# Key products and the two products that join the block inverses put on 64x64 array tiles, in a gated delta network followed by a softplus MLP

## The chip, the core and the metric

One core of one Trainium2 chip runs the whole program. The core has TensorE (PE; loading of its weights is shown as PEld), VectorE (DVE), ScalarE (ACT), GpSimd (POOL) and SyncE (SP, which here only issues transfers). The time is device microseconds from launch to end; lower is better. Times of a kernel are given as the median of its runs; the profile is of one further execution.

## What is computed

```python
def _attn_ref(q, k, v, beta, g):                  # (4, 8, 768, 48); beta (4, 8, 768)
    k_n = k / (np.linalg.norm(k, axis=-1, keepdims=True) + 1e-06)
    state = np.zeros((B, H, D, D))
    for t in range(S):
        readout = np.einsum('bhd,bhde->bhe', q[:, :, t], state)
        y[:, :, t] = g[:, :, t] * readout
        v_old = np.einsum('bhde,bhd->bhe', state, kt)
        state = state + bt[:, :, :, None] * np.einsum('bhd,bhe->bhde', kt, vt - v_old)

def _moe_ref(x, w_in, w_out):                      # x: (3072, 384); d_ff = 2048
    h = x @ w_in
    g = np.maximum(h, 0.0) + np.log1p(np.exp(-np.abs(h)))
    return g @ w_out
```

x is y with the heads side by side. The kernel does the recurrence in chunks of 64 steps: inside a chunk the updates are the solution of a triangular system, so each chunk and head needs the inverse of a 64x64 unit triangular matrix built from the products of its keys.

## The kernel before

**Chunks and pairs.** S = 768 is cut into NC = 12 chunks of C = 64. There are 4 batches by 8 heads = 32 heads in all; a tile holds 64 steps of two batches on its 128 partitions, and a 64x64 array tile serves one head. Inverses are made for two chunks at a time (a pair, `cc` = 0 to 5), 64 triangular matrices in 32x32 blocks.

**Front** (`front(c, ...)`). `load` and `load_q` bring k, q, v, g of a chunk in two halves of 192 KB each (rings `kf`, `qf`, `vf`, `gf` of 4, 3, 4, 3 buffers). k is normalised (`kmul`), k and q are transposed on PE (`trs`), evicted into `kqt` (`kev`). Then come the key products. For chunks 0 and 1 `gramk` (L405, L406) takes key by key alone and `gramq` (L438) key by query; for the others `gram` (L475, L476) takes both in one product, 32 products on 64x32 array tiles for half a chunk. Each 64x64 key product is written with the columns of the lower half swapped, so that the two diagonal 32x32 blocks of every head stand in `kk[:, 0]` and the others in `kk[:, 1]`. `kkc` evicts them, `mask` evicts the query part.

**Inverse** (`inverse(cc, ...)`). DVE transposes the diagonal blocks (`ln`); POOL (DVE for the first pair) makes the inverses of 16x16 blocks in 15 steps of two operations (`step`). `cv` and `tn` bring one of them, `c16` and `t32` both, back to the block form. Two products join 16x16 blocks to 32x32: `xmm` (L665), 64 products of 16x32 by 16x16 for each chunk, evicted by `xs` in one piece for a pair, and `tmm`, which first copies the diagonal with 4 products by the identity (L686) and adds 64 products of 32x16 by 32x16 (L692), evicted by `td2`. `zmm` (L718, L721) joins 32x32 to 64x64.

**Chain** (`chain(c)`). For each chunk and half of the heads: `ks` and `qs` with the state (L759), `w`, `umm` (L802, L806), `u1`, `zu` (L827), `u2`, then `smm` (L847) and `s` for the next state, `ymm` (L877), `y`, `ytr` (L911), `xt`. These products are small, 16 or 18 at a time, on 64x64 or 32x32 array tiles.

**Dense** (`dense(cs)`). `g1` (L941) takes xt by w_in into `h`, `soft` (ACT) applies softplus, `g2` (L968) takes that by w_out into `o`, evicted and stored. A `g1` or `g2` item is 3, 6 or 4 full-array products. The weights (`wload`, POOL's queue, L273) come in eight parts, w0.0 to w0.3 of w_in and w1.0 to w1.3 of w_out.

**Order.** Nothing reorders at run time. `_ORDER` is a list of entries, an engine's letter and an item's number, and every engine executes its items in that order. A ring's slot is given at an item's place in the list, and an item that needs a slot waits until its last user is done; a load that waits holds up all loads and stores behind it on SP. `pow` (L541) on POOL makes the norms of pairs 1 to 5; `ksq` on ACT squares the keys for them.

Of the kernel before, what the change touches and what calls it, by code (L numbers as in the profile page):

```python
# [74 lines left out]
def kernel(  # L75
# [11 lines left out]
    nc = tc.nc  # L87
# [48 lines left out]
    r_kk = ring("kk", 3, [P, 2, U, HC], F16)  # L136
    r_kqt = ring("kqt", 5, [P, 4 * NP * 2 * C + HC], F16)
# [6 lines left out]
    r_tv = ring("tv", 2, [P, 8, HC, 2], F16)  # L144
    r_tn = ring("tn", 2, [P, U, 16], F16)
    r_xs = ring("xs", 2, [P, U, 16], F16)
# [42 lines left out]
    for t in r_kqt.tiles:  # L189
        nc.vector.memset(t[:, 8 * NP * C :], 0.0)  # L190
    pat = pool.tile([P, HC], F16, name="pat")
    nc.vector.tensor_tensor(pat, ident[:, :HC], ident[:, 64 : 64 + HC], ALU.add)
    for t in r_z.tiles:
        nc.vector.tensor_copy(t[:, :, :HC], pat[:, None, :].broadcast_to([P, 16, HC]))
# [84 lines left out]
    def kq_of(c):  # L279
        return kqt[c].ap[:, : 8 * NP * C].rearrange("p (n t) -> p n t", n=4 * NP)  # L280

    def front(c, kk, nv, nv_it):
# [106 lines left out]
        def u_of(ap, p, m):  # L389
            return ap[:, :, 16 * cl + 8 * p + m : 16 * cl + 8 * p + 8 : 2]  # L390
# [4 lines left out]
        if c < 2:  # L395
            gk = [Buf(p_d), Buf(p_d)]
            for p in range(2):

                def gramk(en, p=p):
                    for i in range(NP):  # L400
                        for r in range(2):
                            for m in range(2):
                                x = kq_u(p, i, r, m)[:, :C]
                                o = gk[m].ap.rearrange("p (n t) -> p n t", n=H)
                                nc.tensor.matmul(o[QUAD[2 * r], NP * p + i], x[:, :HC], x)  # L405
                                nc.tensor.matmul(  # L406
                                    o[QUAD[2 * r + 1], NP * p + i],
                                    x[:, HC:],
                                    x.rearrange("f (x t) -> f x t", x=2)[:, ::-1],
                                )  # L410

                t2 = add("gramk", f"{c}.{p}", "P", gramk, deps=[its["k"][p]],
# [703 lines left out]
```

## Time and profile before

| | us |
|---|---|
| median of 3 runs (lowest, highest) | 302.21 (299.0, 303.22) |
| the profiled execution | 303.66 |
| its span, from the first instruction to the last | 301.7 |

The span is 2 us under the profiled execution's time. Rows of the profile name an engine, a line of the kernel, an operation and its tiles; "idle before" is how long the engine sat idle just before, and the name behind the arrow is what ended that; "issue" there means that nothing the profile shows ended it. PEclk is the clock granted to TensorE as a share of full speed: 1.0 is 2.4 GHz, 0.5 is 1.2 GHz.

### The profile page before, as it was taken

To read this page: it belongs to the slowest core of one execution; us is meant where nothing else is said; L and a number is where in the kernel's file an instruction comes from. 1 tells how busy PE (TensorE), PEld (TensorE's weight loads), DVE (VectorE), ACT (ScalarE), POOL (GpSimd) and SP (SyncE) were. 2 spreads that over 40 slices of the span, in tenths; PEclk is the share of its full clock that TensorE was granted. 3 is DMA by queue.
4 is the path that set the end of the run, shared out by engine and by line. 5 is a ranking of instruction groups with operands and counts; after the bars stand their busy time and mean duration, and the time that the engine had idled before them with its cause. 6 is when DMAs were issued, how large, how long until landed. Compare 5 with 4: busy or idle time off the path is not lost.

```text
span 301.7 us, 13385 instructions
## 1 busy us (share of the span) xinstructions
PE 236.7 (78%) x6112; PEld 161.7 (54%) x6112; DVE 141.0 (47%) x307; ACT 131.7 (44%) x239; POOL 119.7 (40%) x217
## 2 busy tenths in 40 slices
PE   1353239869949976989996996998996999999960
PEld 1233137656737833566653566764564556667730
DVE  7689447824824775374680453553433324112000
ACT  3546245743524764562463523265520355334510
POOL 7204809986361882749868500006820000000000
PEclk9999999977978999799997897798997899999995
DMA  8999998999501099530683012841031110011111
GB/s 126 201 179 186 186 182 141 191 202 161 109 4 30 25 168 163 128 83 8 129 148 69 13 43 65 140 93 31 20 88 32 33 50 9 22 45 39 39 50 42
DMA packets 85480, 27.69 MB, mean 92 GB/s; under 512 B 75568, under 2 KB 85424, under 8 KB 85424
## 3 DMA queue, kind: packets, MB, share of 16 engines
q1 hardware_dynamic: 79376, 23.21, 42.2%
q0 software_dynamic: 3968, 3.25, 7.0%
q8 instruction: 47, 0.77, 1.2%
q10 hardware_dynamic: 2080, 0.39, 0.9%
q14 instruction: 9, 0.07, 0.1%
HBM read 25.26 MB, written 4.72 MB: 99 GB/s over the span
## 4 chain that ended last, share of the span: by engine, by line
PE 70%; DMA 10%; issue 9%; SPq 2%; POOL 2%; ACT 2%; DVE 1%; POOLq 0%; ACTq 0%; DVEq 0%
PE h L941 23%; PE o L968 22%; DMA kf<-in_k_dram 5%; PE d L759 4%; DMA beta_l<-in_beta_dram 3%; PE d L877 2%; PE d L827 2%; DMA out_dram<-osb 2%; PE d L665 2%; PE d L847 2%; PE d L692 2%; PE d L321 2%; PE d L911 2%; PE d L475 2%; PE d L721 1%
## 5 line engine op out<-in xcount | busy, mean ns | idle before, releaser
L941 PE MATMUL h<-xt,w_in 128*128 128x512 f16 (+1 forms) x384 | 78.2, 344 | 1.9 <-ACT ga L953 1.9
L968 PE MATMUL o<-w_out,ga 128*128 128x384 f16 x384 | 75.1, 341 | 0.7 <-ACT osb L200 0.6
L953 ACT ACTIVATE ga<-h 128x512 f16<-128x512 f32 x96 | 57.0, 597 | 37.4 <-PE h L941 35.0
L968 PEld LDWEIGHTS <-ga 128*128 128x128 f16 x384 | 37.6, 102 | 26.6 <-issue 4.6
L941 PEld LDWEIGHTS <-w_in 128*128 128x128 f16 x384 | 36.4, 101 | 24.6 <-issue 5.4
L609 POOL TENSOR_TENSOR tt<-tt,tmp 128x30 f32<-128x30 f32 (+7 forms) x75 | 27.7, 369 | 5.9
L541 POOL TENSOR_TENSOR nv<-nv,half_c 128x32 f32<-128x32 f32 x5 | 27.2, 5449 | 6.6 <-DVE nv L524 6.6
L602 POOL TENSOR_TENSOR tmp<-nn,tt 128x30 f32<-128x30 f32 (+7 forms) x75 | 26.5, 353 | 5.4
L200 ACT ACTIVATE u<-d 128x384 f16<-128x384 f32 x30 | 14.3, 490 | 26.3 <-PE d L806 14.6
L592 POOL TENSOR_TENSOR nn<-ln,beta_l 128x256 f32<-128x256 f16 x10 | 6.0, 619 | 42.9 <-DVE ln L574 42.9
L200 ACT ACTIVATE kqt<-d 128x1024 f16<-128x1024 f16 (+1 forms) x18 | 15.5, 877 | 16.2 <-PE d L321 12.2
L303 POOL TENSOR_TENSOR kn<-kf,nv 128x768 f16<-128x768 f32 x8 | 12.5, 1573 | 19.6 <-DVE nv L547 14.5
L200 ACT ACTIVATE osb<-o 128x384 f32<-128x384 f32 x14 | 6.9, 490 | 29.6 <-PE o L968 24.7
L493 DVE TENSOR_TENSOR mt<-d,mask 128x256 f16<-128x256 f32 x40 | 15.4, 411 | 8.8 <-ACT kk L200 5.4
L892 DVE TENSOR_TENSOR yg<-d,gf 128x384 f16<-128x384 f32 x24 | 12.7, 552 | 14.2 <-PE d L877 14.2
L202 DVE COPY osb<-o 128x384 f32<-128x384 f32 x10 | 5.5, 554 | 28.2 <-PE o L968 28.2
L793 DVE TENSOR_TENSOR w<-vf,d 128x384 f16<-128x384 f32 x22 | 11.1, 547 | 15.4 <-PE d L759 15.4
L759 PE MATMUL d<-s,kqt 48*64 48x48 f16 x704 | 16.2, 195 | 2.1 <-issue 2.1
L665 PE MATMUL d<-tn,kk 16*32 16x16 f16 x768 | 8.6, 171 | 11.8 <-issue 10.6
L202 DVE CAST u<-d 128x384 f16<-128x384 f32 x18 | 9.9, 554 | 16.4 <-PE d L806 8.9
L759 PEld LDWEIGHTS <-kqt 48*64 48x64 f16 x704 | 13.4, 115 | 6.3 <-issue 5.9
L524 DVE TENSOR_REDUCE nv<-ksq 128x16 f32<-128x768 f32 x12 | 11.3, 942 | 10.1 <-ACT ksq L520 10.1
(104 smaller groups left out, 361.7 us busy)
## 6 DMA issues: line engine op xcount, KB each, us to landing
qf<-in_q_dram SPq DMA_DIRECT2D x24, 192.0 KB
vf<-in_v_dram SPq DMA_DIRECT2D x24, 192.0 KB
gf<-in_g_dram SPq DMA_DIRECT2D x24, 192.0 KB
out_dram<-osb SPq DMA_DIRECT2D x24, 192.0 KB
kf<-in_k_dram SPq DMA_DIRECT2D x22, 192.0 KB
w_in<-in_moe_w_in_dram POOLq DMA_DIRECT2D x4, 384.0 KB, 9.0
w_out<-in_moe_w_out_dram POOLq DMA_DIRECT2D x4, 384.0 KB, 8.4
kf<-in_k_dram ACTq DMA_DIRECT2D x2, 192.0 KB
```

Of the source, the lines that this page charges most:

```text
L200: nc.scalar.activation(o, x, AF.Copy, scale=float(sign))
L202: ENG[en].tensor_copy(o, x)
L493: nc.vector.tensor_tensor(mt[c][m].ap[:, NP * p : NP * p + NP], gb[m].ap.rearrange("p (n b) -> p n b", n=NP)[:, :, C:], mask[:, None, :].b ...
L541: lambda en: nc.gpsimd.tensor_tensor(nv.ap, nv.ap, half_c, ALU.pow),
L602: eng.tensor_tensor(t, nn.ap[:, :, j + 1 :, j : j + 1].broadcast_to([P, 2, n, w]), tt.ap[:, :, j : j + 1, :w].broadcast_to([P, 2, n, w]), ...
L609: eng.tensor_tensor(rows, rows, t, ALU.add)
L665: nc.tensor.matmul(uv(xp.ap)[QUAD[qd], u], kk.ap[r, 0, u, :], tn.ap[r, u, :])
L759: nc.tensor.matmul(hd(o.ap)[HALF[r], NP * p + i], kq_of(c)[FEAT[m], 8 * p + 2 * i + r, off : off + C], s0[r].ap[FEAT[m], NP * p + i], **st ...
L892: lambda en, m=m: nc.vector.tensor_tensor(heads(yg.ap, m), hd(yp[m].ap), heads(gf.ap, m), ALU.mult),
L941: nc.tensor.matmul(hp.ap[:, n * b : n * b + n], w_in[:, j, f * P : (f + 1) * P], xt.ap[:, j, t0 : t0 + n], start=(j == 0), stop=(j == 2),)
L953: lambda en, hp=hp, o=gb: nc.scalar.activation(o.ap, hp.ap, AF.Softplus),
L968: nc.tensor.matmul(op.ap[:, :DM], b.ap[:, col + c0 : col + c0 + 128], w_out[:, f, :], start=(f == 0), stop=(f == NF - 1),)
```

## The change

- The key products of a half chunk are 16 instead of 32, each the whole 64x64 product of a head (64 weight columns, key and query columns moving: 128 columns) on a 64x64 array tile. `kk` holds them as they are. For pair 0 separate products `gramd` make the diagonal 32x32 blocks from the keys alone (32 for half a chunk, evicted by 8 small `kdc` into `kkd`), and `gram` follows when q is there.
- For pairs 1 to 5 the diagonal blocks are picked out of `kk` by two masked operations over 128x1024: `kd0` (ACT or POOL: left half times a 0/1 column) and `kd1` (DVE: right half times the other column, added). `ln` reads the result.
- `xmm` is 32 products of 64x64 by 64x32 for a chunk. Its operand is the 16x16 inverse written at one of two places with zeros at the other, so `cv` is two masked copies and the transposition `tn` twice as wide (512 columns). `xs` is one eviction for each chunk, masked: one operation on DVE, or two on ACT.
- `tmm` is 32 products of 64x64 by 64x16; a part of `xs` that is set once holds an identity, so the 4 copying products fall away.
- The rings `kf`, `qf`, `vf` have 3, 2, 3 buffers instead of 4, 3, 4; `xs` has 1 instead of 2 (each larger), `kkd` has 1.
- `_ORDER` is a new list. Around pair 1's inverse PE's entries were xmm 2, xmm 3, ks 2.0, qs 2.0, ks 2.1, tmm 3, tmm 2, g2 1.0.0; they are now xmm 3, xmm 2, g1 1.2, trs q6, tmm 3, tmm 2, g2 0.1.0, g2 0.1.4, qs 2.0, zmm 2. On ACT, `ksq` of chunks 4 and 5 stood before the first `z`; now it stands behind the first `u2`, around `xt` 0. On POOL, w0.1 is issued near the head, before any cast; w0.0, w0.2 and w0.3 stand behind `pow` of pair 1, the cast of q3 and `kmul` of chunk 2, where all four stood around that `pow`. On DVE, three masks and a reduction now stand before `tn` of pair 0, where one mask stood. In all PE has 4976 products instead of 6112, by the lists' own counts.

```diff
-    r_k = ring("kf", 4, [P, 2, H, D], F32)
-    r_q = ring("qf", 3, [P, 2, 8, D], F32)
-    r_v = ring("vf", 4, [P, 2, H, D], F32)
+    r_k = ring("kf", 3, [P, 2, H, D], F32)
+    r_q = ring("qf", 2, [P, 2, 8, D], F32)
+    r_v = ring("vf", 3, [P, 2, H, D], F32)
...
-    r_kk = ring("kk", 3, [P, 2, U, HC], F16)
+    r_kk = ring("kk", 3, [P, U, C], F16)
+    r_kkd = ring("kkd", 1, [P, U, HC], F16)
...
-    r_xs = ring("xs", 2, [P, U, 16], F16)
+    r_xs = ring("xs", 1, [P, U, 2, HC], F16)
...
+    for i in range(4):
+        nc.vector.memset(own[QUAD[i], i % 2 : i % 2 + 1], 1.0)
...
+    def scaled(en, o, x, by):
+        if en == "A":
+            nc.scalar.activation(o, x, AF.Copy, scale=by)
+        else:
+            ENG[en].tensor_scalar_mul(o, x, by)
...
+                def gramd(en, p=p):
...
+                                for y in range(2):
+                                    b = x[:, HC * y : HC * y + HC]
+                                    nc.tensor.matmul(o[QUAD[2 * r + y], NP * p + i], b, b)
...
+            def gram(en, p=p, gb=gb):
+                for i in range(NP):
+                    for r in range(2):
+                        for m in range(2):
+                            x = kq_u(p, i, r, m)
+                            o = gb[m].ap.rearrange("p (n b) -> p n b", n=NP)
+                            nc.tensor.matmul(o[HALF[r], i], x[:, :C], x)
...
+        if not raw:
+            def kd0(en):
+                scaled(en, kkd.ap, kk.ap[:, :, :HC], own[:, :1])
+
+            def kd1(en):
+                nc.vector.scalar_tensor_tensor(
+                    kkd.ap, kk.ap[:, :, HC:], own[:, 1:2], kkd.ap, ALU.mult, ALU.add
+                )
...
+        def cvs(en):
+            for x in range(2):
+                scaled(
...
+            def xmm(en, cl=cl, xp=xp):
+                for u in range(16):
+                    for r in range(2):
+                        nc.tensor.matmul(
+                            xp.ap[HALF[r], HC * u : HC * u + HC],
+                            kk.ap[HALF[r], 16 * cl + u],
+                            tn.ap[HALF[r], 16 * cl + u].rearrange("p x j -> p (x j)"),
+                        )
...
+            def xsc(en, cl=cl, xp=xp):
+                o = xs.ap[:, 16 * cl : 16 * cl + 16, :, :16]
+                i = xp.ap.rearrange("p (u x j) -> p u x j", u=16, x=2)
+                if en == "D":
+                    nc.vector.tensor_tensor(
+                        o, i, ownw[:, None].broadcast_to([P, 16, 2, 16]), ALU.mult
+                    )
+                else:
+                    for x in range(2):
+                        scaled(en, o[:, :, x], i[:, :, x], own[:, x : x + 1])
...
             def tmm(en, cl=cl):
-                us = slice(16 * cl, 16 * cl + 16)
-                for qd in range(4):
-                    r = QUAD[qd]
-                    nc.tensor.matmul(
-                        uv(ep.ap)[r, us], ident[r, r], td.ap[r, us, 16:],
-                        start=True, stop=False, skip_group_check=True,
-                    )
                 for u in range(16 * cl, 16 * cl + 16):
-                    for qd in range(4):
+                    for r in range(2):
                         nc.tensor.matmul(
...
+                            uv(ep.ap)[HALF[r], u],
+                            xs.ap[HALF[r], u].rearrange("p x c -> p (x c)"),
+                            td.ap[HALF[r], u, 16:],
```

## Rows read from the trace of the kernel before

**Rows 1.** The page: engines (busy us, share, instructions), instruction queue, chain by engine.

```profile
PE 236.7 (78%) x6112; PEld 161.7 (54%) x6112; DVE 141.0 (47%) x307; ACT 131.7 (44%) x239; POOL 119.7 (40%) x217
...
q8 instruction: 47, 0.77, 1.2%
...
PE 70%; DMA 10%; issue 9%; SPq 2%; POOL 2%; ACT 2%; DVE 1%; POOLq 0%; ACTq 0%; DVEq 0%
```

**Rows 2.** Busy us by stretch: PE, PEld, DVE, ACT, POOL; PEclk; DMA; GB/s.

```profile
0.00:49.06 49.06, 18.67 (x662) 15.24 (x663) 34.33 (x94) 21.04 (x40) 21.80 (x30) 1.00 1.10 172
49.06:291.93 242.87, 218.04 (x5452) 146.47 (x5450) 106.71 (x214) 110.22 (x199) 97.94 (x188) 0.92 0.41 78
291.93:301.70 9.77, 0.00 (x0) 0.00 (x0) 0.00 (x0) 0.49 (x1) 0.00 (x0) 0.64 0.12 43
```

**Rows 3.** PE's waits, 49.06 to 291.93: us in total, times, longest.

```profile
PE d L665 <- issue: 7.3, 3, 2.6
...
PE h L941 <- ACT ga L953: 1.9, 1, 1.9
...
PE d L806 <- issue: 1.4, 1, 1.4
```

**Rows 4.** Timeline of PE, 82 to 93: start us, us, what, count, idle before.

```profile
82.15 1.17 PE L665 MATMUL d<-tn,kk 16*32 16x16 f16 x128
83.25 0.78 PE L759 MATMUL d<-s,kqt 48*64 48x48 f16 x43
86.11 0.25 PE L759 MATMUL d<-s,kqt 48*64 48x48 f16 x5 [2.08 <-issue]
...
89.84 0.24 PE L692 MATMUL d<-td,xs 32*16 32x16 f16 x13 [2.11 <-issue]
90.02 2.74 PE L968 MATMUL o<-w_out,ga 128*128 128x384 f16 x8
```

**Rows 5.** DMA queues, 82.5 to 103.5: packets, MB, share of 16 engines.

```profile
q8 instruction: 6, 0.10, 2.1%
```

**Rows 6.** Busy us by stretch again, columns as in rows 2.

```profile
62.48:65.90 3.42, 3.42 (x77) 3.00 (x76) 1.31 (x3) 1.64 (x4) 2.87 (x8) 0.50 1.34 201
...
229.74:236.55 6.81, 5.09 (x30) 2.94 (x30) 1.90 (x4) 0.00 (x0) 0.00 (x0) 0.50 0.05 19
236.56:291.50 54.94, 54.31 (x867) 36.11 (x866) 11.01 (x22) 25.33 (x45) 0.00 (x0) 1.00 0.12 37
```

**Rows 7.** The chain that ended last, whole span: start us, us, what.

```profile
75.08 0.52 PE d L847 x31
...
79.62 2.60 PE o L968 x16
...
123.47 0.49 PE d L692 x58
```

**Rows 8.** Timeline of PE, 26 to 49, columns as in rows 4.

```profile
26.36 0.81 PE L438 MATMUL d<-kqt 48*64 48x64 f16 x32 [1.45 <-ACT kqt L200]
...
32.75 0.29 PE L665 MATMUL d<-tn,kk 16*32 16x16 f16 x17 [3.27 <-issue]
...
39.22 0.27 PE L692 MATMUL d<-td,xs 32*16 32x16 f16 x17 [4.01 <-issue]
```

**Rows 9.** The chain, 0 to 50, columns as in rows 7.

```profile
27.70 13.30 DMA kf<-in_k_dram
```

**Rows 10.** Groups by line and shape: count, busy us, mean ns, idle before.

```profile
L200 ACT ACTIVATE kqt<-d 128x1024 f16<-128x1024 f16 x12 | 12.2, 1022 | 14.4 <-PE d L321 11.6 <-PE d L364 2.3 <-DVE mt L493 0.3
...
L541 POOL TENSOR_TENSOR nv<-nv,half_c 128x32 f32<-128x32 f32 x5 | 27.2, 5449 | 6.6 <-DVE nv L524 6.6
```

**Rows 11.** SP's waits, whole span: us in total, times, longest.

```profile
SPq L247 <- DVE qn L202: 16.1, 1, 16.1
```

**Rows 12.** Timeline of PE, 116 to 126, columns as in rows 4.

```profile
116.15 0.23 PE L475 MATMUL d<-kqt 48*32 48x128 f16 x1
...
116.50 1.13 PE L665 MATMUL d<-tn,kk 16*32 16x16 f16 x103
```

More of the change, by code (lines that the diff above doesn't have):

```diff
@@ L188 @@
         nc.vector.memset(t, 0.0)
-    for t in r_kqt.tiles:
-        nc.vector.memset(t[:, 8 * NP * C :], 0.0)
     pat = pool.tile([P, HC], F16, name="pat")
     nc.vector.tensor_tensor(pat, ident[:, :HC], ident[:, 64 : 64 + HC], ALU.add)
+    own = pool.tile([P, 2], F32, name="own")
+    ownw = pool.tile([P, 2, 16], F16, name="ownw")
+    nc.vector.memset(own, 0.0)
+    for i in range(4):
+        nc.vector.memset(own[QUAD[i], i % 2 : i % 2 + 1], 1.0)
+    nc.vector.tensor_copy(ownw, own[:, :, None].broadcast_to([P, 2, 16]))
+    id64 = pool.tile([P, 2, HC], F16, name="id64")
+    nc.vector.tensor_tensor(
+        id64.rearrange("p a b -> p (a b)"), ident[:, :64], ident[:, 64:], ALU.add
+    )
+    for t in r_xs.tiles:
+        for i in range(2):
+            nc.gpsimd.tensor_copy(
+                t[:, :, i, 16:], id64[:, i, None, 16:].broadcast_to([P, U, 16])
+            )
     for t in r_z.tiles:
@@ new lines, in front, with kkc, mask_m @@
+        mt_it[c] = [[], []]
+        for p in range(2):
+            gb = [Buf(p_d), Buf(p_d)]
+            def gram(en, p=p, gb=gb):
+                for i in range(NP):
+                    for r in range(2):
+                        for m in range(2):
+                            x = kq_u(p, i, r, m)
+                            o = gb[m].ap.rearrange("p (n b) -> p n b", n=NP)
+                            nc.tensor.matmul(o[HALF[r], i], x[:, :C], x)
+            t2 = add("gram", f"{c}.{p}", "P", gram, deps=its["k"] + its["q"],
+                     bufs=gb + [kqt[c]], mm=16, mode="6464")
+            for m in range(2):
+                def kkc(en, p=p, m=m, gb=gb):
+                    copy(
+                        en,
+                        u_of(kk.ap, p, m),
+                        gb[m].ap.rearrange("p (n b) -> p n b", n=NP)[:, :, :C],
+                        -1,
+                    )
+                def mask_m(en, p=p, m=m, gb=gb):
@@ L549, in norms, with inverse @@
         return add("eps", tag, "D", eps, deps=[root], bufs=[nv], size=not raw)
-    def inverse(cc, kk, kk_it, nv, nv_it):
+    def inverse(cc, kk, kk_it, kkd, kd_it, nv, nv_it):
         tag = f"{2 * cc}"
@@ L572, in inverse @@
         ln, nn, tt, tmp = Buf(r_ln), Buf(r_n), Buf(r_t), Buf(r_tmp)
+        if not raw:
[4 more added lines that the diff above has]
+                    kkd.ap, kk.ap[:, :, HC:], own[:, 1:2], kkd.ap, ALU.mult, ALU.add
+                )
+            kd_it = [add("kd0", tag, "AG", kd0, deps=kk_it, bufs=[kk, kkd])]
+            kd_it = [add("kd1", tag, "D", kd1, deps=kk_it + kd_it, bufs=[kk, kkd])]
         l1 = add("ln", tag, "D",
@@ L690, in tmm @@
+            e4 = add("xs", f"{2 * cc + cl}", "AD", xsc, deps=[e3], bufs=[xp, xs], size=512)
+            def tmm(en, cl=cl):
                 for u in range(16 * cl, 16 * cl + 16):
[L691 removed]
+                    for r in range(2):
                         nc.tensor.matmul(
[L693 to L699 removed]
@@ L997 @@
         nv_it = norms(cs, nv, cc in ON_ACT)
-        kk_it = front(cs[0], kk, nv, nv_it) + front(cs[1], kk, nv, nv_it)
-        inverse(cc, kk, kk_it, nv, nv_it)
+        kkd = Buf(r_kkd)
+        ka, kb = front(cs[0], kk, kkd, nv, nv_it), front(cs[1], kk, kkd, nv, nv_it)
+        inverse(cc, kk, ka[0] + kb[0], kkd, ka[1] + kb[1], nv, nv_it)
     table = add("table", "", "A",
```

317 lines of the change are left out of this document (118 added, 199 removed).

## The prediction

> **What bounds the kernel now.** I read the page first. PE is busy for 78% of the span and holds 70% of the chain that ended last; "issue" holds 9% of it, time in which nothing shown holds PE up [rows 1]. The stages differ, so the windows come next [rows 2]. Up to 49.06 us, where the first dense product starts, PE is busy for 19 us and DMA is saturated (172 GB/s). From 49.06 to 291.93 PE is busy for 218 of 242.9 us, while DVE, ACT and POOL stay under half. The last 9.8 us are the final store and the end. So the middle stage is PE's, and its idle time decides. PE's waits there [rows 3]: eight groups end in "issue", from 7.3 us before xmm (L665) down to 1.4, in sum 21.8 us; waits for ACT are 2.5 us, for anything else nil. PE hardly waits for data; it waits for its own instructions.
>
> The timeline shows how [rows 4]. From 82.15 PE runs 128 xmm products in 1.1 us and 43 ks products, stands for 2.08 us, runs 5 more ks and 123 of tmm's 136 products, 128 in all, and stands for 2.11 us. The two stalls end 3.73 us apart. The instruction queue moved 0.77 MB in 47 blocks for PE's 12,224 instructions [rows 1]: 16.4 KB a block, 63 bytes each, so a block holds about 130 products with their weight loads. Six came between 82.5 and 103.5, one in 3.5 us [rows 5]. I read this as a limit: a block of 128 products can't be followed by another sooner than about 3.7 us. A small product costs 8 to 17 ns [rows 7], so a block of them is used up in 1.1 to 2.2 us and PE stands for the rest; a dense product costs 2.60/16 = 0.163 us [rows 7], so some 12 of them in a block (three items) hide the refill.
>
> The stalls cost a second time. Eight stretches, 40.9 us in all, run at a granted clock of 0.50 (1.2 GHz), the first from 62.48, the last from 229.74 [rows 6], most of them opening at or just behind a stall. In 90.02 to 92.7 eight dense products take 2.74 us [rows 4], 0.33 us each, twice the 0.163. From 236.56 to 291.50 there is no stall and the clock is 1.00 [rows 6]. At most half of the 40.9 us, 20 us, can be lost so; stalls and small products, which need not slow by half, are part of it. I put the loss at 13 us.
>
> **The change part by part.**
>
> *Fewer instructions.* 6112 - 4976 = 1136 products fewer, in the densest places: xmm and tmm of a pair fall from 264 to 128, gram by half. I cut both lists of PE's entries, from the first dense product on, into lots of 128, priced each by the rows (small 8 to 17 ns, dense 0.163 us, a transposition by its 128 columns a third of that) and took what is missing to 3.7 us. Before, about 20 of 44 lots fall short, by 27 us in all, eleven of them by over 1.2; the rows say 21.8, so the count is a fifth too dark. After, 6 to 12 of 36 fall short, by 4 to 8 us depending on where the cut falls, for some cuts one of them by 2 us. The lot from xmm 3 on shows why: it was 128 products without a dense one, and is now 64 xmm, one g1 item, 8 transpositions and part of tmm. I take 6 us left: -16 us (bounds -21.8, all gone, and -8, if the refill is slower than it seems).
>
> *Clock.* With no stall near 2 us, most slow stretches have no cause. 4 of the 13 us stay: -9 us (bounds -13 and -2).
>
> *Array time.* No row shows xmm on 64x64 tiles. Nearest is smm (L847), 31 products 64x64 by 48 columns in 0.52 us, 16.8 ns each [rows 7]; 32 of them are 0.54 us, against 64 old xmm in 0.55 [rows 4]: nothing. tmm: 64 at 0.49/58 = 8.4 ns [rows 7] are 0.54, also the new price; only the four wide identity products go, about 0.15 us, ten times after 49.06: -1.5 us. gram: 32 took 0.35 us [rows 12]; 16 new ones cost 0.27 us by smm's rate, and at most 0.81 us by L438, 32 of 64 columns in 0.81 us [rows 8], half as many and twice as wide. The kernel row with the same tile is nearer, with its columns 2.7 times; I take 0.35, no change, and keep +9 us (20 times 0.46) as a bound. Sum -1.5 us (bounds -7 and +9).
>
> *Longer inverse.* kd0 is a 128x1024 operation, 1.02 us by the eviction of that size on ACT [rows 10]; kd1, by the same row, about 1.1; two masked copies for one, a doubled transposition and xs in two parts about 1.2 more: by my estimate +3.3 us of latency in each pair and, in sum, under 15 us on either engine. The cover is that these engines are busy for 107 and 110 of 242.9 us [rows 2], and that the new list puts a pair's inverse well ahead. Where the cover ends, tmm or zmm waits in PE's order and all chain products stand behind it. Rings of one buffer (xs, kkd) make a pair wait for the one before, whose last use stands far ahead in the list: nothing. New waits in all: +4 us (bounds 0 and +14).
>
> *Start.* xmm of pair 0 followed the products of 26.36 to 27.2 [rows 8]. Now three masks and a reduction stand before tn, and cv doubles: I let it start some 4 us later. Then both stalls, 3.27 and 4.01 us [rows 8], should go, since xmm and tmm of this pair fall from 264 products to 128. Behind them ACT and DVE stood in ksq and its reduction until a key load of 13.30 us landed at 41.0 [rows 9]; now these stand behind u2, and the load is hidden by the chain of chunk 0. Against that, POOL issues w0.0, w0.2 and w0.3 only behind a pow of 5.45 us [rows 10], the cast of q3 and a kmul, at about 40 us by my count; and with two buffers for q SP's next loads wait for that cast. First dense product at 44.5 us: -4.5 us (bounds -8 and +3).
>
> *Sum*: -16 - 9 - 1.5 + 4 - 4.5 = -27 us. The profiled execution, 303.66 us with a span of 301.7, is 1.45 us over the median of 302.21; from the median, 275 us.
>
> From 82.15 PE starts 128 products with their weight loads, a block's worth of instructions, in 1.1 us, and stands for 2.08 us soon after [rows 4]. A rule speaks against my reading: the Trainium skill (Runtime: NRT & Kernel Launch, Instruction fetch mechanics) says that instructions are refilled in 16 KiB blocks and that this stays hidden, because the sequencer dispatches more slowly than blocks arrive. The trace agrees on the block (0.77 MB in 47) and not on the dispatch. By that rule the stalls have another cause and stay: about 300 us, the second rival, instead of 275.
>
> **The rivals.**
>
> 1. *Half the gain.* PE waits for evictions and the longer inverse where it waited for instructions. For: 3.3 us more in each pair, and waits hidden under stalls come out. Against: only 2.5 us of waits for ACT today, and the last 55 us run without any. At half of 27 us: about 289.
>
> 2. *No gain.* The stalls are not a matter of the number of products: another hold-up at such places, such as the switch between tile shapes or the transfers that saturate DMA. Against: exactly 128 products lie between the two stalls shown [rows 4], and the second one falls within tmm, at no switch. Left are array time and start: -6 us and +4, about 300.
>
> 3. *Slower.* The small rings starve PE. SP issues in order; a load that waits for a buffer holds up all behind it, and q already had one such wait of 16.1 us with three buffers [rows 11], which cost PE nothing. If each of chunks 2 to 11 must wait for a load, ten waits must pass 2.7 us each to eat the 27 us, and 3.3 to be slower by 2%; a key load under saturated DMA took 13.30 us [rows 9]. At 3.8 us each: 313. Against: from 49.06 us on DMA is busy for 0.41 of the time [rows 2], and the loads stand far ahead in the list.
>
> **How the numbers follow.** The forecast's case holds 0.62, with its own range 261 to 284; rival 1 0.20 (284 to 294), rival 2 0.11 (296 to 305), rival 3 0.07 (over 308). Low end 261: half of what lies between the terms taken and their best bounds (about 15 of 29 us). High end 292 takes in most of rival 1; below 261 and above 292 lie about 2 in 10. Faster by over 2% means under 296.2: 0.62 + 0.20 = 0.82; within 2%, about what a measurement of this kernel can tell from no change, 0.11; slower 0.07.
>
> **What would show it.** Right: about 38 instruction blocks; PE's "issue" waits after the first dense product at 4 to 9 us, at most one over 1.5; slow-clock stretches under 15 us in sum; the first dense product near 44.5; xmm and gram items no longer than 0.6 and 0.4 us. Wrong: stalls of 2 us remaining with fewer blocks (rival 2); PE idle with ACT or DVE named before tmm, zmm or umm (rival 1); PE, ACT or DVE waiting for kf, qf, vf (rival 3); gram near 0.8 us each. The weakest step is the new list: each engine's order is fixed, and a single late item holds its queue.

## The result

| | before | after |
|---|---|---|
| median of 4 runs (lowest, highest), us | 302.72 (299.0, 303.91) | 274.65 (272.9, 276.37) |
| ratio, 95% interval | | 0.911 (0.9 to 0.9219) |
| the profiled execution, us | 303.66 | 274.83 |
| its span, us | 301.7 | 273.1 |

A ratio compares the fast runs of both kernels alone, so it can differ a little from the quotient of the medians. Forecast were 275.0 us and a range of 261 to 292. The page of the changed kernel, engines, instruction queue and chain as in [rows 1]:

```profile
PE 226.6 (83%) x4976; PEld 155.3 (57%) x4976; DVE 147.4 (54%) x304; ACT 146.1 (54%) x277; POOL 135.5 (50%) x229
...
q8 instruction: 39, 0.64, 1.0%
...
PE 50%; POOL 14%; DVE 12%; DMA 11%; issue 5%; ACT 2%; SPq 1%; DVEq 0%; ACTq 0%; POOLq 0%
```

39 instruction blocks came instead of 47, and PE is the chain for half of the span only; POOL, DVE and DMA have taken the rest. The windows of the changed kernel, columns as in [rows 2]: the start, PE's stage, the end, and the only two stretches of slow clock ahead of the end:

```profile
0.00:42.72 42.72, 19.93 (x574) 16.81 (x575) 34.38 (x97) 23.36 (x51) 23.87 (x34) 1.00 0.94 153
42.72:260.42 217.70, 206.66 (x4404) 138.53 (x4402) 113.00 (x208) 122.30 (x225) 111.64 (x195) 0.98 0.49 94
260.42:273.10 12.68, 0.00 (x1) 0.00 (x0) 0.00 (x0) 0.49 (x1) 0.00 (x0) 0.70 0.12 45
125.56:128.97 3.41, 3.41 (x30) 1.84 (x23) 1.66 (x2) 1.92 (x4) 3.41 (x1) 0.50 0.98 190
200.65:204.06 3.41, 3.41 (x16) 1.84 (x14) 0.70 (x2) 0.81 (x1) 0.00 (x0) 0.50 0.00 0
```

PE's waits of the changed kernel in its stage, from 42.7 us on, columns as in [rows 3]:

```profile
PE d L660 <- DVE tn L620: 2.2, 1, 2.2
PE d L749 <- ACT kk L214: 2.1, 1, 2.1
PE d L901 <- DVE yg L882: 2.0, 2, 1.8
PE d L456 <- issue: 1.0, 1, 1.0
PE d L749 <- issue: 0.7, 1, 0.7
```

With [rows 2, 3] this says where the 28.6 us of span went (waits are summed over all lines of the view):

| us | before | after | difference |
|---|---|---|---|
| up to the first dense product | 49.06 | 42.72 | -6.3 |
| PE's stage, first dense product to PE's end | 242.87 | 217.70 | -25.2 |
| of it PE's waits that end in "issue" | 21.8 | 2.1 | -19.7 |
| of it PE's waits for other engines | 2.5 | 8.6 | +6.1 |
| of it PE busy | 218.04 | 206.66 | -11.4 |
| behind PE's last product | 9.77 | 12.68 | +2.9 |

The 49.06 us of [rows 2] is where the chain enters the first dense product of the kernel before; in PE's timeline it starts at 48.90. By the timeline of both kernels the start is 6.2 us shorter and the stage 25.3.

The eight stretches of slow clock, 40.9 us, have become two, 6.8 us. These are the recorded ones. The trace holds no record of the clock ahead of 48.8 us before and of 47.0 us after, so the 1.00 of the first windows is no measurement, and PE works there at half pace: the first six dense products of the changed kernel take 1.49 us, six later ones 0.83. From 42.72 to 47.0 that is another 4.3 us at half pace, some 11 us in all. Timeline of PE, columns as in [rows 4]:

```profile
42.72 1.49 PE L931 MATMUL h<-xt,w_in 128*128 128x256 f16 x6
...
73.41 0.83 PE L931 MATMUL h<-xt,w_in 128*128 128x256 f16 x6
```

More rows of that timeline show the new products: both xmm items of a pair in 1.19 us, where 128 old ones took 1.17 [rows 4]; tmm's 64 in 1.18; a gram item in 0.42 to its last end.

```profile
72.29 1.19 PE L660 MATMUL d<-tn,kk 64*64 64x32 f16 x64 [2.24 <-DVE tn L620]
...
74.61 1.18 PE L685 MATMUL d<-td,xs 64*64 64x16 f16 x64
...
120.52 0.42 PE L456 MATMUL d<-kqt 48*64 48x128 f16 x16
```

### The profile page after: what moved, and what is told of

It is laid out like the page before. It is cut to its first block, busy times and chain, and to the rows that moved or that the text cites. A ratio compares the mean times of both kernels' runs of the same rounds, so it can differ in the third digit from the quotient of the medians.

```text
span 273.1 us, 11156 instructions
## 1 busy us (share of the span) xinstructions
PE 226.6 (83%) x4976; PEld 155.3 (57%) x4976; DVE 147.4 (54%) x304; ACT 146.1 (54%) x277; POOL 135.5 (50%) x229
## 4 chain that ended last, share of the span: by engine, by line
PE 50%; POOL 14%; DVE 12%; DMA 11%; issue 5%; ACT 2%; SPq 1%; DVEq 0%; ACTq 0%; POOLq 0%
PE o L958 17%; PE h L931 15%; DMA kf<-in_k_dram 5%; POOL tmp L592 4%; POOL tt L599 4%; DMA gf<-in_g_dram 3%; PE d L749 3%; DMA out_dram<-osb 2%; POOL nv L519 2%; PE d L341 2%; PE d L867 2%; DVE tt L599 2%; PE d L817 2%; PE d L901 1%; PE d L685 1%
## 5 line engine op out<-in xcount | busy, mean ns | idle before, releaser
L931 PE MATMUL h<-xt,w_in 128*128 128x512 f16 (+1 forms) x384 | 73.2, 329 | 0.4 <-ACT ga L943 0.4
L958 PE MATMUL o<-w_out,ga 128*128 128x384 f16 x384 | 72.9, 336 | 0.6 <-ACT osb L214 0.6
L519 POOL TENSOR_TENSOR nv<-nv,half_c 128x32 f32<-128x32 f32 x5 | 27.3, 5469 | 4.5 <-DVE nv L502 4.5
L214 ACT ACTIVATE kqt<-d 128x1024 f16<-128x1024 f16 (+1 forms) x22 | 19.2, 886 | 5.8 <-PE d L384 4.5
L471 DVE TENSOR_TENSOR mt<-d,mask 128x256 f16<-128x256 f32 x48 | 18.6, 416 | 5.7 <-ACT kk L214 3.4
L214 ACT ACTIVATE kk<-d 128x256 f16<-128x256 f32 x38 | 13.5, 387 | 13.3 <-DVE mt L471 10.7
L456 PE MATMUL d<-kqt 48*64 48x128 f16 x384 | 12.6, 242 | 9.4 <-ACT kk L214 4.5
L749 PEld LDWEIGHTS <-kqt 48*64 48x64 f16 x704 | 13.0, 108 | 8.8 <-issue 8.6
L216 DVE CAST u<-d 128x384 f16<-128x384 f32 x15 | 8.2, 553 | 18.2 <-PE d L817 14.4
L456 PEld LDWEIGHTS <-kqt 48*64 48x64 f16 x384 | 8.4, 118 | 14.4 <-issue 13.6
L341 PE MATMUL d<-ident,kn 128*128 128x128 f16 x96 | 9.1, 250 | 6.7 <-DVE kn L216 6.5
L498 ACT ACTIVATE ksq<-kf 128x768 f32<-128x768 f32 x12 | 10.1, 843 | 8.3 <-DMA kf<-in_k_dram 8.1
```

The lines of the kernel that those rows point to most:

```text
L341: nc.tensor.transpose(o[:, p, i], kx.ap[:, p, 2 * i : 2 * i + 2].rearrange("p h d -> p (h d)"), ident,)
L456: nc.tensor.matmul(o[HALF[r], i], x[:, :C], x)
L471: nc.vector.tensor_tensor(mt[c][m].ap[:, NP * p : NP * p + NP], gb[m].ap.rearrange("p (n b) -> p n b", n=NP)[:, :, C:], mask[:, None, :].b ...
L519: lambda en: nc.gpsimd.tensor_tensor(nv.ap, nv.ap, half_c, ALU.pow),
L749: nc.tensor.matmul(hd(o.ap)[HALF[r], NP * p + i], kq_of(c)[FEAT[m], 8 * p + 2 * i + r, off : off + C], s0[r].ap[FEAT[m], NP * p + i], **st ...
L931: nc.tensor.matmul(hp.ap[:, n * b : n * b + n], w_in[:, j, f * P : (f + 1) * P], xt.ap[:, j, t0 : t0 + n], start=(j == 0), stop=(j == 2),)
```

## The experiments

All kernels in one table; the ratio is to the kernel before, timed on the same chip in the same rounds. The columns behind it are from each one's profiled execution: the first dense product, PE's last end, and, between them, waits that end in "issue", waits for other engines, and recorded time at a clock of 0.50. The records begin up to 4.3 us behind the first dense product, and until then PE works at half pace. e4_even, e9_order2 and e10_stores ran on another chip than the rest, which is why the ratio counts. The profiled executions of e3_rings (276.8 us), e11_ksq_rings (278.5) and e4_even (285.3) were the longest of their runs, so that their columns stand for a longer execution than the median.

| kernel | median us | ratio (95%) | first dense | PE's end | issue | other waits | slow clock |
|---|---|---|---|---|---|---|---|
| before | 302.72 | | 48.9 | 291.93 | 21.8 | 2.5 | 40.9 |
| after | 274.65 | 0.911 (0.9, 0.9219) | 42.72 | 260.42 | 2.1 | 8.6 | 6.8 |
| e2_half | 275.79 | 0.9141 (0.9048, 0.9234) | 48.3 | 264.1 | 8.8 | 4.8 | 13.6 |
| e1_split | 294.98 | 0.9743 (0.9627, 0.9858) | 45.3 | 280.7 | 9.9 | 2.8 | 17.1 |
| e4_spread | 291.1 | 0.9642 (0.9566, 0.9718) | 42.8 | 275.7 | 1.6 | 3.4 | 0 |
| e4_bunch | 291.52 | 0.9651 (0.9567, 0.9736) | 44.2 | 276.9 | 4.7 | 4.1 | 27.3 |
| e4_even | 283.32 | 0.9405 (0.9328, 0.9481) | 44.0 | 270.9 | 4.2 | 4.1 | 13.7 |
| e5_ksq | 282.64 | 0.9296 (0.9215, 0.9377) | 49.9 | 267.3 | 0 | 8.8 | 13.6 |
| e11_ksq_rings | 275.65 | 0.9176 (0.9051, 0.9302) | 44.4 | 264.1 | 0.2 | 8.4 | 20.5 |
| e6_short | 273.32 | 0.9008 (0.8937, 0.9079) | 42.2 | 258.1 | 1.9 | 8.0 | 6.8 |
| e3_rings | 274.7 | 0.9013 (0.892, 0.9106) | 42.9 | 262.4 | 1.9 | 8.4 | 13.6 |
| e8_order | 269.69 | 0.8908 (0.8816, 0.9) | 42.2 | 257.7 | 1.6 | 6.5 | 10.2 |
| e9_order2 | 266.23 | 0.8834 (0.8782, 0.8887) | 42.5 | 255.5 | 2.6 | 5.0 | 6.8 |
| e10_stores | 261.2 | 0.8669 (0.8618, 0.8719) | 42.5 | 256.2 | 2.9 | 4.9 | 6.8 |

### Is it the number of products?

The kernel before, with half as many products; order, rings and evictions are untouched:

```diff
-                for u in range(16 * cl, 16 * cl + 16):
+                for u in range(16 * cl, 16 * cl + 16, 2):
...
-                            uv(xp.ap)[QUAD[qd], u], kk.ap[r, 0, u, :], tn.ap[r, u, :]
+                            uv(xp.ap)[QUAD[qd], u : u + 2], kk.ap[r, 0, u, :], tn.ap[r, u : u + 2, :]
...
+                                if i % 2:
+                                    continue
...
-                                nc.tensor.matmul(o[QUAD[2 * r], i], x[:, :HC], x)
-                                nc.tensor.matmul(o[QUAD[2 * r + 1], i], x[:, HC:C], y)
+                                u0 = 8 * p + 2 * i + r
+                                y = kq_of(c)[FEAT[m], u0 : u0 + 3 : 2]
+                                nc.tensor.matmul(o[QUAD[2 * r], i : i + 2], x[:, :HC], y)
+                                nc.tensor.matmul(o[QUAD[2 * r + 1], i : i + 2], x[:, HC:C], y)
```

(tmm, gramk and gramq in the same way.)

> The kernel before, its order, rings and evictions, with half as many xmm, tmm and key products: each pair of neighbours is one product with the first one's weights and twice the moving columns (the second one's results are wrong). 1,184 products fewer (4928). Theory (number of products): the stalls go without any new order; issue waits after the first dense product from 21.8 us to under 8, 275 to 286 us. Rival (order): the stalls stay where they are, 295 to 303 us.

275.79 us, 0.9141: the old list, old rings and old inverse lose 27 us when the products are halved, as much as the whole change. Its instruction queue on the page:

```profile
q8 instruction: 38, 0.62, 0.9%
```

PE's longest waits in its stage, columns as in [rows 3]:

```profile
PE d L764 <- issue: 4.5, 3, 2.9
PE d L697 <- issue: 2.6, 2, 1.7
PE h L946 <- ACT ga L958: 2.0, 1, 2.0
```

Issue waits fall from 21.8 to 8.8 us (the theory said under 8), slow clock from 40.9 to 13.6. The order has no part in that. Merged products also spend less of the array's time (an xmm item 0.37 us where the old one took 0.57, tmm 0.38 where it took 0.70; PE is busy for 219.2 us in the span, against 226.6 in the changed kernel). Some 5 us of the 27 are that, and the equality of the two times is partly chance.

The traces also show the refill itself. The packets of the instruction queue are in them, with the time at which each block of 16 KB landed. All 64 "issue" waits of PE behind 30 us, in the 14 kernels of this document, end 1.2 to 1.7 us after such a landing (the median is 1.45), 16 of 16 in the kernel before: its stalls that end at 86.11 and 89.84 [rows 4] follow blocks that landed at 84.71 and 88.43, 1.40 us each. And of 579 blocks no two start closer together than 3.36 us.

The reverse, the changed kernel with its products cut in two:

```diff
-                            nc.tensor.matmul(o[HALF[r], i], x[:, :C], x)
+                            for y in range(2):
+                                ys = slice(C * y, C * y + C)
+                                nc.tensor.matmul(o[HALF[r], i, ys], x[:, :C], x[:, ys])
```

(xmm and tmm in the same way, over 16 and 8 columns.)

> The changed kernel, order and all, with each of the three kinds of products cut in two again: gram into 64 + 64 columns, xmm into 16 + 16, tmm into 8 + 8, same weights, same results. That puts 1,152 products back (4976 to 6128, before had 6112). Theory (PE's instructions run dry: a block of 128 small products is used up faster than the next arrives): most stalls come back, with the slow clock behind them; 289 to 299 us, PE's issue waits after the first dense product 12 to 20 us, some 47 instruction blocks. Rival (the new order, or larger tiles, took the stalls away, not the number): only array time is added, 275 to 282 us, issue waits under 6 us.

294.98 us: 20 of the 28 us are gone again, with the new list and rings in place. Issue waits rise from 2.1 to 9.9 us, fewer than the 12 to 20 expected, slow clock from 6.8 to 17.1. Its instruction queue on the page:

```profile
q8 instruction: 48, 0.79, 1.1%
```

PE's longest waits for "issue" in its stage:

```profile
PE d L458 <- issue: 4.6, 3, 3.1
PE d L841 <- issue: 1.6, 1, 1.6
```

The rest is array time, which I had put too low. PE is busy for 222.1 us in its stage, 15.4 more than in the changed kernel; at most 5 of these are the 10.3 us more of slow clock, so some 10 us are products: on a 64x64 tile one costs about 16 ns even with 16 or 8 columns, where the old small tiles cost 8.4 [rows 7]. Slower products also leave more time for a refill. So this run shows that stalls come back with the number; their price is better read from e2_half.

### Number or density?

Three kernels add small products that change nothing in the results, ahead of each g1 item, ahead of xmm, or ahead of zu and smm:

```diff
             def g1(en, f0=f0, hp=hp):
+                for y in range(8):
+                    nc.tensor.matmul(hp.ap[HALF[y % 2], :16], ident[HALF[y % 2], HALF[y % 2]], ident[HALF[y % 2], :16])
```

> The changed kernel with 768 small products added (64x64 by 16 columns, into a buffer that is overwritten right after, so the results stay): 8 ahead of each of the 96 g1 items, among dense products. Both theories: their array time only, 768 by 8 to 17 ns = 6.5 to 13 us, so 281 to 288 us, issue waits as in the changed kernel (2.1 us) or up to 5.

> The same 768 products, but in twelve lots of 64 ahead of xmm, where small products already stand together. Theory (a block of 128 can't be followed by another sooner than 3.7 us): each pair of chunks then has 192 small products in a row and stands for 1.5 to 3 us: 6.5 to 13 us of array time, 9 to 15 us of stalls, some slow clock: 292 to 303 us, at least 8 us longer than with the same products spread. Rival (number of instructions doesn't matter): the same time as spread, 281 to 288 us.

291.1 and 291.52 us: the 8 us between them did not show, and spread was 3 us above its range. Equal times, with different causes. Timeline of PE of the spread kernel, 251 to 258, columns as in [rows 4]:

```profile
255.02 0.29 PE L929 MATMUL h<-ident 64*64 64x16 f16 x8
255.24 0.83 PE L933 MATMUL h<-xt,w_in 128*128 128x256 f16 x6
255.91 0.81 PE L960 MATMUL o<-w_out,ga 128*128 128x384 f16 x4
256.65 0.29 PE L929 MATMUL h<-ident 64*64 64x16 f16 x8
```

From start to start a lot of 8 takes 0.22 us, 28 ns a product. The dense product just ahead of it takes 93 ns more than its neighbours, too (256 ns against 163 for 384 columns): the four from 255.91 need 0.74 us to the next lot's start, where 0.65 is usual. By the 0.22 alone 96 lots are 21 us, and PE is busy for 21.0 us more than in the changed kernel; the time rose by only 16.5, since the waits for other engines fell from 8.6 to 3.4. There is no stall of note, and no record of the clock, from 46.9 us on, shows it below full speed. In the bunched kernel, 72 to 83:

```profile
72.86 1.18 PE L659 MATMUL d<-ident 64*64 64x16 f16 x64
73.89 0.66 PE L662 MATMUL d<-tn,kk 64*64 64x32 f16 x32
74.40 1.12 PE L659 MATMUL d<-ident 64*64 64x16 f16 x61
77.79 0.23 PE L659 MATMUL d<-ident 64*64 64x16 f16 x3 [2.27 <-issue]
...
82.87 2.74 PE L960 MATMUL o<-w_out,ga 128*128 128x384 f16 x8
```

64 products take 1.03 us from start to start, 16 ns each; 157 small ones run in a row; then PE stands for 2.27 us, and from 77.03 to 90.69 the clock is 0.50: eight dense products take 2.74 us, as in [rows 4]. Its stalls came to 4.7 us, not to the 9 to 15 expected, and the time lies just under its range. The count of lots by 3.7 us a block put the stalls too high here as in the forecast (27 against 21.8, 6 against 2.1) and in e1_split (12 to 20 against 9.9); only e2_half went a little the other way. To take the change of tile shape out of the comparison, the third kernel sets the products among others of the same tile:

> The changed kernel with 736 small products added (64x64 by 16 columns), 16 ahead of each zu and of each smm: small products beside small products of the same array tile, but never more than 34 in a row more than before. In the runs with 768 spread among dense products or bunched at xmm, the time was the same (291.1 and 291.5), but the first paid in array time (0.30 us for each lot of 8, at a full clock), the second in stalls (4.7 us) and slow clock (27.3 us). Theory (cost of a lot: its array time at some 15 ns a product when no change of tile shape is added, and stalls only where 128 come in under 3.7 us): 11 us of array time, issue waits 2 to 6 us, slow clock under 14 us: 284 to 289 us. Rival (each added product costs the same 21 ns wherever it stands): 290 to 292 us.

283.32 us, 8 us under the bunched kernel with 32 products fewer, intervals apart; the theory's end, and a little below its range. Issue waits are nearly the same (4.2 and 4.7 us); the bunched kernel has 13.6 us more of slow clock. PE is busy for 218.5 us in its stage, against 223.7 in the bunched one. So crowding costs, and here it does so through the clock more than through the stalls themselves.

### What won the start?

The changed list with the squares of chunks 4 and 5 in their old place. Nothing but the list differs:

```
ACT before the edit: ..., w0 0.1, z 0, u1 0.1, z 1, u2 0.1, u2 0.0, ksq 4, xt 0.0, xt 0.1, ksq 5, ...
ACT after it:        ..., w0 0.1, ksq 4, ksq 5, z 0, u1 0.1, z 1, u2 0.1, u2 0.0, xt 0.0, xt 0.1, ...
SP: loads k4, k5 ahead of them; DVE: red 4, red 5 behind them
```

> The changed kernel with one step of the new order undone: the key loads of chunks 4 and 5, ksq 4, ksq 5 and their two reductions stand ahead of z 0 again, as in the kernel before. Theory of the forecast (the start is won by hiding that load behind the chain of chunk 0): the first dense product comes 3 to 5 us later than 42.7, at 46 to 48, and the time is 277 to 280 us. Rival (the start is won by the two stalls that went, and the squares wait beside them anyway): first dense product within 1 us of 42.7, 273 to 276 us.

282.64 us, first dense product at 49.9, 7.2 us later: more than expected (46 to 48). SP's waits from 10 to 50 us, columns as in [rows 11]:

```profile
SPq L245 <- DVE kn L323: 12.1, 1, 12.1
```

ACT's timeline, 30 to 52, columns as in [rows 4]:

```profile
41.78 0.84 ACT L498 ACTIVATE ksq<-kf 128x768 f32<-128x768 f32 x1 [5.10 <-DMA kf<-in_k_dram]
```

PE's timeline, the same stretch:

```profile
43.54 0.62 PE L817 MATMUL d<-u,z 64*64 64x48 f16 x16 [6.38 <-ACT u L214]
```

SP stood 12.1 us for a key buffer, until the kmul of k3 (L323) was done; the load came late, ACT stood in ksq, z and u stood behind it, and PE 6.4 us behind u. The ring of three keys had a part in that, so the last run gave this list the old rings of loads:

```diff
-    r_k = ring("kf", 3, [P, 2, H, D], F32)
-    r_q = ring("qf", 2, [P, 2, 8, D], F32)
-    r_v = ring("vf", 3, [P, 2, H, D], F32)
+    r_k = ring("kf", 4, [P, 2, H, D], F32)
+    r_q = ring("qf", 3, [P, 2, 8, D], F32)
+    r_v = ring("vf", 4, [P, 2, H, D], F32)
...
```

(To make room, `kk`, `z`, `u16` and `s16` lose 1, 1, 2 and 1 buffers.)

> The list with ksq 4 and ksq 5 ahead of z 0 (282.6 us, first dense product at 49.9), and the load rings of the kernel before on top (kf 4, qf 3, vf 4; kk 2, z 3, u16 4, s16 5). With three key buffers SP waited 12.1 us, until kmul of k3, to issue the load of k5, and DMA stood still from 28 to 40 us. Theory A (the place of the squares costs by itself): first dense product still at 46 to 50, 278 to 283 us. Theory B (it costs only because three buffers make that load late; the new place of the squares is what pays for the smaller ring): the load lands before 36 us, first dense product at 42 to 45, 273 to 278 us.

First dense product at 44.4, 275.65 us: theory B. Of the 7.2 us, 5.6 are the small ring, 1.6 the place of the squares. With e3_rings, below, which has the changed list and the old rings (42.9), four kernels form a square: the old place of the squares costs 1.5 us with the old rings and 7.2 with the small ones, and in the changed list the small rings cost nothing at the start. In ACT's timeline of this kernel ksq 5 now waits for no load, only for the reduction before it:

```profile
37.67 0.84 ACT L498 ACTIVATE ksq<-kf 128x768 f32<-128x768 f32 x1 [1.37 <-DVE nv L502]
```

And the two stalls of 3.27 and 4.01 us [rows 8] were not what held the start. In e2_half, with the old list, they are gone, and the first dense product comes at 48.3 all the same; ACT's timeline of e2_half:

```profile
41.46 0.84 ACT L525 ACTIVATE ksq<-kf 128x768 f32<-128x768 f32 x1 [4.48 <-DMA kf<-in_k_dram]
```

The key load of [rows 9], at 41 us, was the bound beside them. From 48.9 to 42.7 us, then: products 0.6, squares 1.6. The remaining 4.0 lie between e2_half and e11_ksq_rings, and I put them down to the rest of the new list, in which this load lands before ACT asks for it. That is a difference of two kernels that differ in more than the list (the longer inverse is one of these things), and which entry does it was not tried.

### The longer inverse and the rings

```diff
-                scaled(en, kkd.ap, kk.ap[:, :, :HC], own[:, :1])
+                pass
...
-                     kkd.ap.bitcast(F32).rearrange("p u t -> p t u"),
+                     (kkd.ap if raw else kk.ap[:, :, :HC]).bitcast(F32).rearrange("p u t -> p t u"),
```

(kd1, the second copy of cv and the masks of xs on ACT are left out as well.)

> The changed kernel without the operations that the larger tiles need: kd0 and kd1 left out (ln reads the left half of kk), one copy instead of two in cv, one unmasked xs instead of two masked on ACT. Products and order stay; the inverses are wrong. Each pair's inverse is some 3 us shorter. Forecast (new waits cost 4 us in all, bounds 0 and 14): 268 to 273 us; what can go by the changed kernel's rows is the 2.2 us wait of xmm 3 for tn, about 1 us of the start and some slow clock behind them. Rival (all of it hidden): 274 to 276 us. Rival (the longer inverse is dear): 261 to 266 us.

273.32 us, 1.3 under the changed kernel by the medians, 3 by the ratios, which overlap: the longer inverse costs between nothing and some 3 us. The next run, e3_rings, was timed in the same rounds and has the same ratio with the longer inverse in place, which speaks for the low end, unless the larger rings gained as much. PE's waits in its stage show the one for tn (2.2 us before) down to 1.1; the two for late loads stand (2.1 and 1.9 us):

```profile
PE d L898 <- DVE yg L879: 2.1, 1, 2.1
...
PE d L658 <- DVE tn L618: 1.1, 1, 1.1
```

The rings alone (the same edit as above, in the changed list):

> The changed kernel with the load rings of the kernel before: kf 4, qf 3, vf 4 instead of 3, 2, 3 (kk 2 instead of 3, z 3 instead of 4, u16 4 instead of 6, s16 5 instead of 6 make the room). Rival of the forecast (small rings make loads late): the waits for k10 (landed at 122) and g9 (landed at 199) shrink, 267 to 271 us. Theory (those loads are late because of their place in SP's list, behind stores, and the rings are large enough): 273 to 276 us, both waits as before.

274.7 us; the ratios overlap, and the waits before ytr (2.5 us) and ks (2.2 us) stand as before. By the medians the small rings cost nothing in this list, by the ratios up to some 3 us; no wait of the trace shows such a cost.

### Can the new waits be had out of the list?

```
SP:  load k10.0, k10.1 from behind load q11.0 to behind load v5.0 (ahead of store 1.1)
SP:  load g9.0 from behind load v11.0 to behind load g9.1
SP:  store 9.1 from behind store 10.1 to behind o 9.1
PE:  xmm 3, xmm 2, g1 1.2, trs q6, tmm 3, tmm 2, g2 0.1.0, g2 0.1.4, qs 2.0, zmm 2
 ->  g1 1.2, xmm 3, xmm 2, g2 0.1.0, g2 0.1.4, trs q6, tmm 3, tmm 2, g2 0.1.8, qs 2.0, zmm 2
```

> The changed kernel with eight entries of its list moved and nothing else: both loads of k10 to just ahead of the store they were queued behind on SP; the second load of g9 directly behind the first; one g1 item ahead of xmm 3, two g2 items between xmm 2 and tmm 3, one ahead of zmm 2; store 9.1 directly behind its eviction. Theory (the three data waits of 2.0 to 2.2 us, the slow clock behind two of them and the queue of four stores at the end are faults of order only): 6 us of waits, 2 to 3 us of slow clock and 2 to 3 us of tail go, 263 to 267 us. Rival (other waits come out where these go): 270 to 275 us.

269.69 us, 5 us of the 8 to 12 expected. The waits for k10 and g9 went, and another came out. PE's waits in the stage:

```profile
PE d L456 <- DVE w L783: 2.6, 3, 2.1
PE d L660 <- DVE tn L620: 1.6, 1, 1.6
```

DVE's waits of this kernel from 110 to 130, and then SP's from 90 to 130:

```profile
DVE w L783 <- DMA vf<-in_v_dram: 4.2, 1, 4.2
```

```profile
SPq L245 <- DVE z L216: 9.4, 1, 9.4
```

k10, now ahead of the store, held SP for 9.4 us until its buffer was free, and v5.1 behind it came late to w. Whether a fourth key buffer would have saved this was not tried. Mended:

```
SP:  load v5.1 directly behind load v5.0; load k10.0, k10.1 behind store 1.1
PE:  g1 1.2, g2 0.1.0, xmm 3, xmm 2, g2 0.1.4, g2 0.1.8, trs q6, tmm 3, tmm 2, g2 0.1.12, qs 2.0, zmm 2
ACT: o 0.0 directly behind g2 0.0.12
```

> The list with eight entries moved, mended where new waits came out: SP waited 9.4 us for a buffer for k10, and v5.1, queued behind it, landed at 122 and held DVE. Now v5.1 stands directly behind v5.0, k10 behind store 1.1; and at pair 1 a g1 and a g2 item stand ahead of xmm 3, two g2 items between xmm 2 and tmm 3. Theory: the waits at 71 (1.6 us) and 122 (2.1 us) and slow clock behind them go, 264 to 268 us. Rival (another wait comes out): 268 to 272 us.

266.23 us, 0.8834: 8 us under the changed kernel by the list alone, intervals apart. A 2.0 us wait for yg now stands before an xmm. The last edit cuts the stores of chunk 11:

```diff
+                    if c == NC - 1:
+                        for b in range(2):
+                            (nc.sync, nc.scalar)[b].dma_start(
+                                out=out[r0 + 2 * S * b : r0 + 2 * S * b + C, :],
+                                in_=ob.ap[64 * b : 64 * b + 64],
+                            )
+                        return
```

> The same list, and each of the last two stores (chunk 11) cut in two halves of 96 KB, one issued by SP, one by ACT. Theory (the end is two stores of some 4 us one behind the other on one queue): 2 to 3 us shorter than with whole stores, the end 6 us behind PE's last product instead of 8.8. Rival (the transfers share what moves them): within 1 us.

261.2 us, 5 us less than with whole stores. The end of both kernels, e9_order2 first, columns as in [rows 2]:

```profile
255.52:264.40 8.88, 0.01 (x1) 0.00 (x0) 0.00 (x0) 0.49 (x1) 0.00 (x0) 0.73 0.11 43
```

```profile
256.23:260.60 4.37, 0.00 (x0) 0.00 (x0) 0.00 (x0) 0.49 (x1) 0.00 (x0) 0.96 0.17 47
```

The end takes 4.4 instead of 8.9 us, and my theory of the queue was not what the trace shows. Busy share of the core's 16 DMA engines in tenths and GB/s, 40 slices from 252 us to the end, e9_order2 first:

```profile
DMA  1011111111111111111111111111111111110000
GB/s 40 30 35 50 55 50 50 50 50 50 50 50 50 50 50 50 50 50 55 50 55 50 50 40 50 50 50 50 50 50 50 50 50 55 50 45 0 0 0 0
```

```profile
DMA  1200120111117799111100000002989300000000
GB/s 14 50 7 36 43 36 14 50 57 43 57 43 200 186 279 329 64 50 50 43 21 0 0 0 0 0 0 57 221 171 343 122 0 0 0 0 0 0 0 0
```

A whole store runs at 50 GB/s with a tenth of the engines' time (0.11 to 0.12 in the windows of the end, two engines of 16), some 4 us for 192 KB; the halves run at up to 343 GB/s on seven to nine tenths. A rule of the Trainium skill (DMA: Bandwidth & Descriptors, Why a DMA increments its semaphore by 16 and not by 1) fits: the number of engines is the largest up to 16 that divides the slowest dimensions of both sides of the transfer. In the whole store these are the pair of batches, 2, and 128 partitions, which makes 2 engines; in a half, 64 steps and 64 partitions, which makes 16. The trace agrees, about two engines against most of them. The halves also go through two queues instead of one; whether one would have done as well was not tried. This version beats both kernels of the case: 0.8669 of the time before.

## Why the prediction was right, step by step

**What bounds the kernel.** Right. Half the products in the old list (e2_half) take off as much as the whole change, some 5 us of it by array time. Rival 2 falls with that run, and with it, for this kernel, the rule of the Trainium skill (Runtime: NRT & Kernel Launch, Instruction fetch mechanics) that the refill stays hidden: 1,184 products fewer took 13 us of issue waits away, with order, rings and evictions untouched, and every one of these waits ends behind the landing of a block.

**Fewer instructions**, -16 taken: -19.7 measured. The count of lots left 6 us of stalls; 2.1 are left. The size was off by 4, within its bounds: the count is too dark by more than the fifth that the forecast allowed it.

**Clock**, -9 taken: about -8.5. Each product that starts in slow clock, priced against the mean of its kind at full clock, makes some 14 us lost before (13 taken) and some 5.5 after (4 taken), 3.4 of them in the two recorded stretches and 2.2 ahead of 47.0 us.

**Array time**, -1.5 taken: about -1.7. Items with neither a wait nor slow clock inside take, from their start to the next item's, 0.57 us before and 0.58 after for xmm, 0.70 and 0.57 for tmm with its identity products, 0.35 and 0.33 for gram (medians of 7 and 10, 4 and 10, 16 and 15 such items; ten, ten and twenty there are). All three are as said, and gram did not come near its bound of 0.81 us. Clock and array time together are 10.2 of the 11.4 us by which PE's busy time in its stage fell; where the last 1.2 went stays open.

**New waits**, +4 taken: +6.1 measured, and the mechanism named was the smaller part. Only the 2.2 us before xmm 3 are the longer inverse, and taking the added work out brought 1.3 us (e6_short). The other two are loads that stood too far back in SP's list. For k10, ACT's timeline of the changed kernel, 108 to 130, columns as in [rows 4], shows ACT in ksq; kk stands behind it, and ks on PE behind kk:

```profile
123.15 0.84 ACT L498 ACTIVATE ksq<-kf 128x768 f32<-128x768 f32 x1 [3.54 <-DMA kf<-in_k_dram]
```

The other is g9, ahead of yg. Both waits went when the entries were moved (e8_order). The forecast had asked of rival 3 whether a buffer would be free in time; what counted was the place in the queue, since larger rings left both waits as they were (e3_rings). The rings showed a price where the list did not suit them: 5.6 us in e5_ksq.

**Start**, -4.5 taken: -6.2 measured. xmm of pair 0 began 3.6 us later (30.68 against 27.10), as taken. But the step that booked the two stalls as gain was wrong: they lay beside the key load that landed at 41, and their going gave 0.6. The squares gave 1.6, and 4.0 are what is left for the rest of the list; and moving the squares is what makes three key buffers bearable.

**Missing term.** The end was taken as unchanged and grew by 2.9 us. store 9.1 stands behind store 10.1 in the new list, so that SP's last row holds four stores in 7.7 us, where it held three; with that store moved the end took 8.8 us (e8_order). The timeline of the last 20 us, before and then after:

```profile
285.22 7.74 SPq L987 DMA_DIRECT2D out_dram<-osb  x3
```

```profile
253.85 7.69 SPq L977 DMA_DIRECT2D out_dram<-osb  x4
```

So the sum of -27 against the measured -28.1 has errors that cancel: the refill and the start gained 4 and 2 us more than taken, the waits and the end took 2 and 3 back; array time and clock came out nearly as taken. The median fell within 0.4 us of the forecast by luck; the range is what the working supports. Two of its figures do not come out of its own rows. The best bounds lie 22.8 us from the terms taken, not 29, so that half of it would have put the low end at about 264 instead of 261; nothing hung on that. And the six blocks of [rows 5] start 3.84 us apart on average, not 3.5, which agrees better with the limit of 3.7 read beside it.

**The signs named.** Blocks 39 (said 38). Issue waits 2.1 us (4 to 9), none over 1.5. Slow clock 6.8 us in the records, some 11 with the half pace ahead of them (under 15). First dense product at 42.7 (44.5). xmm 0.58 and gram 0.33 us (0.6 and 0.4). Of the wrong signs, PE waited once for DVE before a join product, and for late kf and gf, 2 us each: the beginning of rivals 1 and 3, too small to decide.

## What to carry to other kernels

Where PE stands with nothing to wait for, count its products between two stalls and compare with the blocks of the instruction queue; and see whether a block lands just ahead of each stall's end; if so, fewer and larger products are worth more than their array time says, and setting them apart is worth something too. After a new order, go through each shared queue for itself: what stands ahead of each late load, and which buffer it asks for; a stall that is removed pays only if nothing ends beside it. And look at how the last stores are laid out: the end of this kernel was worth 4.5 us for a few lines.

## What the runs showed of the hardware

PE stood until a block of its instruction queue had landed: 64 of 64 "issue" waits end 1.2 to 1.7 us after a landing, and no two blocks start closer than 3.36 us. On 16x32 or 32x16 tiles 128 products are used up in 1.1 us [rows 4], on 64x64 tiles 64 take 1.03 (e4_bunch).

A lot of 8 products on 64x64 tiles between dense ones cost 28 ns a product from start to start, 16 ns in a lot of 64: each change to the small tiles and back costs some 0.1 us behind it, and the dense product ahead of it takes 93 ns longer (e4_spread).

Nearly every slow stretch goes with a standstill of PE, be it for instructions or for data. Of the 40 that the records of the 14 kernels show ahead of PE's end, 39 open within some 2 us of a wait of 0.57 to 3.07 us, or contain one near their start; one, from 151.74 in e1_split, has none. In the changed kernel the clock falls just behind the waits that end at 124.32 and 200.48, which are for data; with no wait over 1.3 us (e4_spread) no record shows it fall. But not every wait brings it: the 2.2 us for tn at 72.29 have no slow stretch behind them in the changed kernel, 6.8 us in e5_ksq and 13.7 in e11_ksq_rings. What decides was not found.

A store whose slowest dimension is 2 moves 50 GB/s, in halves of 64 rows up to 343; all stores but the last two of e10_stores still go the slow way, which no wait of PE shows there.
